# Gated FFN after a long convolution: gate activations written over the product's buffer, front loads on other queues, a row add on GpSimd

## The chip, the cores and the metric

One Trainium2 chip, one of its cores. The time is the device time of one execution in microseconds, as the median of several runs. The engines are PE (matrix products), ACT (activations, and reads of PSUM), DVE (elementwise work), POOL (GpSimd: here small elementwise work and DMA issues) and SP (DMA issues alone). Every engine works through its own list of instructions in order and waits for the others on semaphores.

## The reference

```python
def _A_ref(q, k, v, shift_k, ssm_k, ssm_D):          # B, S, D = 1, 2048, 640
    k_shift = sum over t < 4 of k shifted by t, times shift_k[:, t]
    kv = k_shift * v
    y = causal long convolution of kv with ssm_k, along S, by FFT of length 2 S
    y = y + kv * ssm_D
    return q * y

def _B_ref(x, w_gate, w_up, w_down):                 # F = 1728
    return (silu(x @ w_gate) * (x @ w_up)) @ w_down

h = A_q + _A_ref(layernorm(A_q), A_k, A_v, A_shift_k, A_ssm_k, A_ssm_D)
out = h + _B_ref(layernorm(h), B_w_gate, B_w_up, B_w_down)
```

## The kernel before

The sequence is cut into four blocks j = 0 to 3 of 512 rows, held as four rows b per partition, and the channels into two halves c of 320. Each block goes through the convolution half by half, then a layer norm, then the FFN. `block_j` (L1151) says the work of one block.

**Convolution.** `kv_block` (L926) makes kv on DVE: eight instructions of 128x1280 per half, on loads kin (of A_k) and vin (of A_v). `k_natural` (L621) transposes the filter: twelve PE transposes at L633 (called ktr below) of the load kraw (of A_ssm_k), one evacuation of 1280 columns, and for block 0 one add of a 320-element row, ssm_D, into the filter's first row (L640, called dadd): that is the skip term. Block 0 uses dense tables (`dense_c`, L690, tables den loaded in pieces by SP). Its forward products on PE are df (with an evacuation each), its inverse products di. Blocks 1 to 3 use a two-stage transform: s1 and s2 on PE (`fwd`, with a shuffle by DMA in between), products of spectra on DVE (`products`), an inverse i2 on PE (`inv2`), again a shuffle by DMA, and the last inverse i1 in `conv_bp` (L1009), which also multiplies by q, adds x and takes the statistics of the layer norm. Block j multiplies spectra of all blocks up to j, so the DVE work grows with j.

**Layer norm of h.** `ln_dve` aggregates the statistics on DVE, `ln_rstd` (L859) finds the inverse root; for j > 0 by fourteen Newton instructions of 128x4 and a last product at L887, all on POOL. `norm` (L890) writes the normalised rows, and `ln_bp` (L1056) transposes them with twenty PE instructions at L1068 (called tr).

**FFN.** `ffn_pair` (L1093) works on two of the 14 feature blocks of F: ten matmuls of 512 columns for the gate (tile pg) and ten for the up projection (tile pu). ACT applies SiLU to pg into the SBUF tile sg (L1107), and DVE multiplies pu by sg into GUT. In the last pair gate and up of the half-filled feature block share one group, so that it has ten matmuls and five. pg and pu come out of one PSUM pool, pF, of two slots; sg has one slot. `ffn_b` (L1130) does the down projection of a row group b, as three pieces of matmuls of 320 columns into PSUM of the same pool (called dn), evacuates and stores it.

**What sets the order.** Nothing is issued in the order of the code. `Prog.schedule` (L104) simulates the five engines with a cost for each operation, takes on each engine the ready operation of lowest priority number, and hands out pool slots as they come free. The lists it makes are the program. Every DMA is put on the list of a named engine, and its landing is set by `dma_model` (L1188), which keeps a clock for the transfers of SP and ACT and another, `bulk`, for those of POOL. An operation may reserve a tile that it doesn't write: it is then scheduled only once that tile has a slot, but its engine doesn't wait for it. The gate groups reserve sg in this way, and the up groups reserve the cells of GUT.

**Names of a step.** A number after a name is block, half, and piece: ktr01 is block 0, half 1; dn125 is block 1, row group 2, feature blocks from 5; i221h2 is the inverse of block 2, half 1, piece 2.

## Time and profile before

| | |
|---|---|
| median of 3 runs | 372.04 us (370.67 to 372.58) |
| the profiled execution's own time | 370.17 us |
| its span, first to last instruction | 368.4 us |
| PE busy | 314.0 us, 85% |
| DVE busy | 223.6 us, 61% |
| ACT busy | 205.8 us, 56% |
| POOL busy | 65.6 us, 18% |
| granted TensorE clock, mean | 0.943 |

All times below are from the start of the span. A timeline row gives start, duration, engine, line, operation, output and input with their shapes, and how many instructions it merges; the bracket at its end is the idle time of the engine before it, and what ended it. q after an engine's name means that its sequencer issued a DMA.

### The profile page before, as it was taken

To read this page: it belongs to the slowest core of one execution; us is meant where nothing else is said; L and a number is where in the kernel's file an instruction comes from. 1 tells how busy PE (TensorE), PEld (TensorE's weight loads), DVE (VectorE), ACT (ScalarE), POOL (GpSimd) and SP (SyncE) were. 2 spreads that over 40 slices of the span, in tenths; PEclk is the share of its full clock that TensorE was granted. 3 is DMA by queue.
4 is the path that set the end of the run, shared out by engine and by line. 5 is a ranking of instruction groups with operands and counts; after the bars stand their busy time and mean duration, and the time that the engine had idled before them with its cause. 6 is when DMAs were issued, how large, how long until landed. Compare 5 with 4: busy or idle time off the path is not lost.

```text
span 368.4 us, 5392 instructions
## 1 busy us (share of the span) xinstructions
PE 314.0 (85%) x2005; PEld 168.1 (46%) x2024; DVE 223.6 (61%) x365; ACT 205.8 (56%) x322; POOL 65.6 (18%) x145
## 2 busy tenths in 40 slices
PE   2599786699999999599888998669998999877993
PEld 0267452345445566244333664244453565333561
DVE  1388787867777785768989968741873701221200
ACT  4278989966676652877763555488763233122111
POOL 3222244361111007000510000600410020000000
PEclk9999998689999999789999999559999999999997
DMA  8997558605414213421200323402001011000011
GB/s 236 359 366 233 157 192 238 224 36 183 130 51 156 97 66 106 155 78 42 96 0 2 117 63 125 162 36 107 2 36 37 0 37 36 2 0 0 0 37 36
DMA packets 22013, 37.16 MB, mean 101 GB/s; under 512 B 2616, under 2 KB 17363, under 8 KB 21988
## 3 DMA queue, kind: packets, MB, share of 16 engines
q1 hardware_dynamic: 16116, 19.51, 14.9%
q0 software_dynamic: 3968, 15.98, 13.8%
q10 hardware_dynamic: 1904, 1.34, 1.3%
q8 instruction: 16, 0.26, 0.3%
q14 instruction: 9, 0.07, 0.1%
HBM read 22.40 MB, written 2.62 MB: 68 GB/s over the span
## 4 chain that ended last, share of the span: by engine, by line
PE 71%; ACT 12%; DMA 4%; POOL 3%; issue 3%; DVE 3%; ACTq 1%; DVEq 0%; POOLq 0%
PE ps L549 68%; ACT sb L534 4%; ACT sb L1107 4%; PE ps L633 3%; DMA sb<-in_A_ssm_k_dram 3%; ACT sb L895 3%; DVE sb L754 2%; DMA sb<-sb 1%; ACTq L542 1%; PE ps L1068 1%; POOL stt L880 1%; POOL stt L879 1%; ACT sb L914 1%; POOL sb L542 1%; POOL stt L881 1%
## 5 line engine op out<-in xcount | busy, mean ns | idle before, releaser
L549 PE MATMUL ps<-sb 128*128 128x320 bf16 (+3 forms) x1207 | 229.4, 338 | 18.8 <-ACT sb L1107 11.2
L754 DVE TENSOR_TENSOR sb<-sb 128x1280 bf16<-128x1280 bf16 (+2 forms) x250 | 161.2, 686 | 35.1 <-ACT sb L534 11.6
L549 PEld LDWEIGHTS ps<-sb 128*128 128x128 bf16 (+2 forms) x1226 | 113.8, 98 | 116.8 <-issue 17.4
L534 ACT ACTIVATE sb<-ps 128x640 bf16<-128x640 f32 (+2 forms) x155 | 109.3, 740 | 86.5 <-PE ps L549 67.3
L549 PE MATMUL ps<-sb,tab 128*64 128x320 bf16 (+2 forms) x622 | 79.8, 330 | 14.6 <-ACT sb L534 9.1
L754 DVE TENSOR_TENSOR sb<-ps,sb 128x1024 bf16<-128x1024 f32 (+3 forms) x44 | 44.4, 1016 | 56.1 <-ACT sb L1107 28.3
L549 PEld LDWEIGHTS ps<-sb,tab 128*64 128x64 f16 (+2 forms) x622 | 39.4, 106 | 54.0 <-issue 21.7
L1107 ACT ACTIVATE sb<-ps 128x1024 bf16<-128x1024 f32 (+2 forms) x32 | 29.3, 917 | 50.7 <-PE ps L549 50.1
L895 ACT ACTIVATE sb<-sb,stt 128x320 bf16<-128x320 bf16 (+1 forms) x42 | 27.8, 710 | 4.4 <-POOL stt L887 3.5
L537 ACT ACTIVATE sb<-ps 128x640 bf16<-128x640 f32 x24 | 16.1, 699 | 10.1 <-PE ps L549 9.8
L633 PE MATMUL ps<-sb 128*128 128x128 bf16 (+1 forms) x96 | 13.7, 240 | 8.3 <-DMA sb<-in_A_ssm_k_dram 8.3
L874 POOL TENSOR_SCALAR stt<-stt 128x4 f32<-128x4 f32 x6 | 2.6, 428 | 84.3 <-DVE stt L856 42.4
L633 PEld LDWEIGHTS ps<-sb 128*128 128x128 bf16 (+1 forms) x96 | 8.6, 117 | 14.8 <-DMA sb<-in_A_ssm_k_dram 9.0
L542 POOL DMA_DIRECT2D sb<-in_A_v_dram x6 | 4.7, 780 | 54.4 <-PE ps L549 53.2
L852 DVE BATCH_NORM_STATS2 stt<-sb 128x6 f32<-128x320 bf16 x32 | 14.0, 480 | 0.0
L542 POOL DMA_DIRECT2D sb<-in_A_ssm_k_dram x12 | 7.7, 647 | 31.3 <-PE ps L633 31.3
L914 ACT ACTIVATE sb<-sb,stt 128x640 bf16<-128x640 bf16 x16 | 13.2, 824 | 0.0
L1068 PE MATMUL ps<-sb 128*128 128x128 bf16 x80 | 7.4, 269 | 6.4 <-ACT sb L537 5.0
L907 ACT ACTIVATE sb<-sb 128x640 bf16<-128x640 bf16 x16 | 11.8, 736 | 0.0
L1068 PEld LDWEIGHTS ps<-sb 128*128 128x128 bf16 x80 | 6.5, 123 | 8.0 <-ACT sb L537 5.9
L542 POOL DMA_DIRECT2D sb<-in_A_k_dram x6 | 5.8, 975 | 19.0 <-DVE sb L754 17.4
L894 DVE TENSOR_SCALAR sb<-sb,stt 128x640 bf16<-128x640 bf16 x6 | 2.5, 443 | 10.3 <-POOL stt L887 10.3
(30 smaller groups left out, 64.5 us busy)
## 6 DMA issues: line engine op xcount, KB each, us to landing
sb<-sb SPq DMA_DIRECT2D x72, 160.0 KB, 2.2
sb<-in_A_k_dram POOLq DMA_DIRECT2D x6, 560.0 KB, 4.9
out_dram<-sb SPq DMA_DIRECT2D x16, 160.0 KB, 1.8
sb<-cst_den SPq DMA_DIRECT2D x9, 256.0 KB, 8.7
sb<-in_B_w_gate_dram POOLq DMA_DIRECT2D x5, 416.0 KB, 4.2
sb<-in_B_w_up_dram POOLq DMA_DIRECT2D x5, 416.0 KB, 4.3
sb<-in_A_q_dram POOLq DMA_DIRECT2D x3, 640.0 KB, 4.8
sb<-in_A_v_dram POOLq DMA_DIRECT2D x6, 320.0 KB, 3.5
```

The lines of the kernel that those rows point to most:

```text
L534: fns = {"act": lambda a: a.activation(out=dst(), in_=src(), func=ACTF.Copy), "dve": lambda v: v.tensor_copy(out=dst(), in_=src())}
L537: fns = {"act": lambda a: a.activation(out=dst(), in_=src(), func=ACTF.Copy, scale=scale), "dve": lambda v: v.tensor_scalar(out=dst(), in0 ...
L542: fns = [(lambda g, d=d, s=s: g.dma_start(d(), s())) for d, s in subs]
L549: return lambda t: t.matmul(o(), l(), r(), start=st, stop=sp)
L633: return t.transpose(B16(pt, b // 2, (b % 2) * CW + d * 128, pr), src, V(IDN, 0, pr, 0, pr))
L754: return lambda v: v.tensor_tensor(out=o(), in0=a(), in1=b_(), op=op)
L852: vec(dve1(CW, False), lambda v: v.bn_stats(st6(l, j, b, c), V(xt, b * D + c * CW, CW)), [(xt, (b, c))], [(ST, ("s", l, j, b, c))], prio, ...
L895: "act": lambda a: a.activation(out=dst(), in_=src(), func=ACTF.Identity, scale=rs(l, j, b), bias=tmv(l, j, 3)[:, b:b + 1])},
L907: P.op({"act": act_c(D) + 0.22}, lambda a, b=b, jt=jt: a.activation(out=V(jt, 0, D), in_=V(xt, b * D, D), func=ACTF.Copy, accum_out=tmv(l, ...
L914: P.op({"act": act_c(D) + 0.3}, lambda a, b=b, jt=jt: a.activation(out=V(jt, 0, D), in_=V(xt, b * D, D), func=ACTF.Square, bias=tmv(l, j, ...
L1068: fns.append(lambda t, k=k, d=d: t.transpose(B16(pt, k, d * 128, 128), V(hn[k], d * 128, 128), V(IDN, 0, 128)))
L1107: P.op({"act": act_c(n)}, lambda a: a.activation(out=dst(), in_=src(), func=ACTF.Silu), rd, wr, -1000, name=f"si{j}{i}")
```

## The change

**The buffer.** The pool of sg is gone. SiLU writes its result straight into the cells of GUT that the product will fill, and the product is formed in place. The gate groups reserve those cells, the up groups nothing.

**The loads.** vin of both halves of block 0 moves from ACT's list to SP's, and kraw of the second half too. The load of x for block 1 (640 KB, on POOL) now comes after the last DVE instruction of the first `kv_block`.

**The row add.** dadd moves from DVE to POOL.

**The model.** `dma_model` has one clock for all large transfers, at 370 KB per us, and a fixed cost for the shuffles. It moves no instruction by itself, but it gives other landing times, so the lists of all engines come out otherwise.

```diff
...
@@ -507,7 +507,6 @@
         P.pool("P0", [HNT.base + i * 2 * CW for i in range(4)], True)
         P.pool("EP", slots(4, 2 * CW), True)
         P.pool("JK", slots(1, 2 * CW), True)
-        P.pool("SG", slots(1, 1024), True)
         P.pool("pF", [0, 1024])
         P.pool("pC", [2048, 3072])
 
@@ -599,7 +598,7 @@
                 subs = [rows(0, 128)]
             dma(subs, 573, [], [(kt, 0)], prio, name=f"kin{j}{c}", eng="pool" if j else "sp")
             dma([(lambda: V2(vt, 0, CW, 4, CW), lambda: dram(V2d, B * j * D + c * CW, [[R * D, 128], [D, 4], [1, CW]]))],
-                328, [], [(vt, 0)], prio + 1, name=f"vin{j}{c}", eng="pool" if j else "act")
+                328, [], [(vt, 0)], prio + 1, name=f"vin{j}{c}", eng="pool" if j else "sp")
 
         def load_kraw(j, c, prio):
             if (j, c) == (0, 1):
@@ -609,12 +608,12 @@
             base = c * CW * S + B * j
             dma([(lambda: V2(t, 0, B, 2, B), lambda: dram(A_ssm_k, base, [[S, 128], [128 * S, 2], [1, B]])),
                  (lambda: V(t, 2 * B, B, 0, 64), lambda: dram(A_ssm_k, base + 256 * S, [[S, 64], [1, B]]))],
-                328, [], [(t, 0)], prio, name=f"kraw{j}{c}", eng="pool" if j else "act")
+                328, [], [(t, 0)], prio, name=f"kraw{j}{c}", eng="pool" if j else ("sp" if c else "act"))
 
         def load_x(j, prio):
             t = xts[j] = P.tile(f"x{j}", "XH")
             dma([(lambda: V(t, 0, 4 * D), lambda: dram(X2, B * j * D, [[R * D, 128], [1, R * D]]))], 655, [],
-                [(t, (b, c)) for b in range(4) for c in range(2)], prio, name=f"x{j}", eng="pool" if j else "sp")
+                [(t, (b, c)) for b in range(4) for c in range(2)], prio, name=f"x{j}", eng="pool" if j else "sp", after=[kv_last[0, 0]] if j == 1 else ())
 
         kts = {}
 
@@ -637,9 +636,9 @@
             evac(lambda: V2(kt, 0, 2 * CW, 2, 2 * CW), lambda: B16x2(pt, 2 * CW), 4 * CW, [(pt, 0)], [(kt, 0)], prio, fast=True,
                  name=f"kte{j}{c}")
             if j == 0:
-                vec(0.25, lambda v: v.tensor_tensor(out=V(kt, 0, CW, 0, 1), in0=V(kt, 0, CW, 0, 1),
-                                                    in1=V(DROW, c * CW, CW, 0, 1), op=ALU.add),
-                    [(DROW, 0), (kt, 0)], [(kt, 0)], prio, name="dadd")
+                P.op({"pool": 1.0}, lambda g: g.tensor_tensor(out=V(kt, 0, CW, 0, 1), in0=V(kt, 0, CW, 0, 1),
+                                                              in1=V(DROW, c * CW, CW, 0, 1), op=ALU.add),
+                     [(DROW, 0), (kt, 0)], [(kt, 0)], prio, name="dadd")
 
         def fwd(nm, srcs, pool, prio):
 
@@ -1094,7 +1093,6 @@
             fbs = (2 * i, 2 * i + 1)
             last = fbs[1] == 13
             g, u = P.tile("pg", "pF"), P.tile("pu", "pF")
-            sg = P.tile("sg", "SG")
             hr = [(HNT, (d, bp)) for d in range(5) for bp in range(2)]
 
             def group(t, bank, w, st, col, cell, prio, reserve):
@@ -1110,22 +1108,22 @@
                 vec(dve1(n), tt(dst, src, sgv, ALU.mult), rd, wr, -1000, name=f"gm{j}{i}")
 
             f0, f1 = fbs
-            group(g, 0, WG, FM, f0 * 128, 0, pf + 4 * i, [(sg, 0)])
+            group(g, 0, WG, FM, f0 * 128, 0, pf + 4 * i, [(GUT, f0)])
             if not last:
-                group(g, 1, WG, FM, f1 * 128, 1, pf + 4 * i + 1, [(sg, 1)])
-                group(u, 0, WU, FM, f0 * 128, 0, pf + 4 * i + 2, [(GUT, f0)])
-                group(u, 1, WU, FM, f1 * 128, 1, pf + 4 * i + 3, [(GUT, f1)])
-                silu(lambda: V2(sg, 0, 512, 2, 512), lambda: B32x2(g, 512), 1024, [(g, 0), (g, 1)], [(sg, 0), (sg, 1)])
-                mul(lambda: V2(GUT, f0 * 512, 512, 2, 512), lambda: B32x2(u, 512), lambda: V2(sg, 0, 512, 2, 512), 1024,
-                    [(u, 0), (u, 1), (sg, 0), (sg, 1)], [(GUT, f0), (GUT, f1)])
+                group(g, 1, WG, FM, f1 * 128, 1, pf + 4 * i + 1, [(GUT, f1)])
+                group(u, 0, WU, FM, f0 * 128, 0, pf + 4 * i + 2, [])
+                group(u, 1, WU, FM, f1 * 128, 1, pf + 4 * i + 3, [])
+                silu(lambda: V(GUT, f0 * 512, 1024), lambda: B32x2(g, 512), 1024, [(g, 0), (g, 1)], [(GUT, f0), (GUT, f1)])
+                mul(lambda: V2(GUT, f0 * 512, 512, 2, 512), lambda: B32x2(u, 512), lambda: V2(GUT, f0 * 512, 512, 2, 512), 1024,
+                    [(u, 0), (u, 1), (GUT, f0), (GUT, f1)], [(GUT, f0), (GUT, f1)])
             else:
-                group(g, 1, GUL, 128, 0, 1, pf + 4 * i + 1, [(sg, 1), (GUT, f1)])
-                group(u, 0, WU, FM, f0 * 128, 0, pf + 4 * i + 2, [(GUT, f0)])
-                silu(lambda: V(sg, 0, 512), lambda: B32(g, 0, 512), 512, [(g, 0)], [(sg, 0)])
-                silu(lambda: V(sg, 512, 512, 0, 64), lambda: B32(g, 1, 512, 64, 128), 512, [(g, 1)], [(sg, 1)])
-                mul(lambda: V(GUT, f1 * 512, 512, 0, 64), lambda: B32(g, 1, 512, 0, 64), lambda: V(sg, 512, 512, 0, 64), 512,
-                    [(g, 1), (sg, 1)], [(GUT, f1)])
-                mul(lambda: V(GUT, f0 * 512, 512), lambda: B32(u, 0, 512), lambda: V(sg, 0, 512), 512, [(u, 0), (sg, 0)], [(GUT, f0)])
+                group(g, 1, GUL, 128, 0, 1, pf + 4 * i + 1, [(GUT, f1)])
+                group(u, 0, WU, FM, f0 * 128, 0, pf + 4 * i + 2, [])
+                silu(lambda: V(GUT, f0 * 512, 512), lambda: B32(g, 0, 512), 512, [(g, 0)], [(GUT, f0)])
+                silu(lambda: V(GUT, f1 * 512, 512, 0, 64), lambda: B32(g, 1, 512, 64, 128), 512, [(g, 1)], [(GUT, f1)])
+                mul(lambda: V(GUT, f1 * 512, 512, 0, 64), lambda: B32(g, 1, 512, 0, 64), lambda: V(GUT, f1 * 512, 512, 0, 64), 512,
+                    [(g, 1), (GUT, f1)], [(GUT, f1)])
+                mul(lambda: V(GUT, f0 * 512, 512), lambda: B32(u, 0, 512), lambda: V(GUT, f0 * 512, 512), 512, [(u, 0), (GUT, f0)], [(GUT, f0)])
 
         def ffn_b(j, b, pf):
             xt = xts[j]
@@ -1185,17 +1183,17 @@
             block_j(j)
 
 
+        link = [1.4]
+
         def dma_model(o, issued, dmafree):
             kb, shuffle = o.dma
-            if o.eng == "pool":
-                s = max(issued + 1.2, bulk[0])
-                bulk[0] = s + kb / 200.0
-                return bulk[0] + 1.1
-            s = max(issued + 0.9, dmafree[0])
-            dmafree[0] = s + kb / (150.0 if shuffle else 330.0)
-            return dmafree[0] + 1.1
-
-        bulk = [0.0]
+            if shuffle:
+                s = max(issued + 0.4, dmafree[0])
+                dmafree[0] = s + 0.55
+                return s + 2.2
+            s = max(issued + (1.2 if o.eng == "pool" else 0.8), link[0])
+            link[0] = s + kb / 370.0
+            return link[0] + 1.0
 
         P.schedule(0.12, dma_model, 1.0)
         if _INFO is not None:
```

The lists stand here at three places, before and after. Lines of the changed kernel are lower by one or two. First POOL at the front, before: the load of x for block 1, then kraw of block 1 (two transfers), kin of block 1, the first weights, vin.

```order
L595 MEMSET sb 1x960 x2
L542 DMA sb<-in_A_q_dram 128x2560
L542 DMA sb<-in_A_ssm_k_dram 128x2x512
L542 DMA sb<-in_A_ssm_k_dram 64x512
L542 DMA sb<-in_A_k_dram 128x7x320
L542 DMA sb<-in_B_w_gate_dram 128x1664
L542 DMA sb<-in_B_w_up_dram 128x1664
L542 DMA sb<-in_A_v_dram 128x4x320
```

The first thing that POOL does after the memsets is the load of x for block 1. The changed list, from the same memset:

```order
L594 MEMSET sb 1x960 x2
L541 DMA sb<-in_A_ssm_k_dram 128x2x512
L541 DMA sb<-in_A_ssm_k_dram 64x512
L639 ISA
L639 TENSOR_TENSOR sb<-sb 1x320
L541 DMA sb<-in_A_k_dram 128x7x320
L541 DMA sb<-in_B_w_gate_dram 128x1664
L541 DMA sb<-in_B_w_up_dram 128x1664
L541 DMA sb<-in_A_q_dram 128x2560
L541 DMA sb<-in_A_v_dram 128x4x320
```

The load of x has moved behind the first weights; ISA (a change of POOL's library) and the first dadd stand behind kraw of block 1.

The second place is PE in the FFN of block 3, its last two pairs; s_act is ACT's semaphore and s_dve that of DVE. Before:

```order
L549 MATMUL ps<-sb 128x512 [waits s_act]
L549 MATMUL ps<-sb 128x512 x9
L549 MATMUL ps<-sb 128x512 [waits s_dve]
L549 MATMUL ps<-sb 128x512 x9
L549 MATMUL ps<-sb 128x512 [waits s_act]
L549 MATMUL ps<-sb 128x512 x4
L549 MATMUL ps<-sb 128x512 [waits s_dve]
L549 MATMUL ps<-sb 128x512 x9
L549 MATMUL ps<-sb 128x320 [waits s_dve]
```

The group of five is the last up group, so up stands ahead of gate in each pair from the second on: the up group waits for the SiLU of the pair before, the gate group for its product. The changed list at the same place:

```order
L548 MATMUL ps<-sb 128x512 [waits s_act]
L548 MATMUL ps<-sb 128x512 x9
L548 MATMUL ps<-sb 128x512 [waits s_dve]
L548 MATMUL ps<-sb 128x512 x9
L548 MATMUL ps<-sb 128x512 [waits s_act]
L548 MATMUL ps<-sb 128x512 x9
L548 MATMUL ps<-sb 128x512 [waits s_dve]
L548 MATMUL ps<-sb 128x512 x4
L548 MATMUL ps<-sb 128x320 [waits s_act,s_dve]
```

Gate now stands ahead of up, the group of five is the last, and each gate group waits for the SiLU of the pair before, each up group for its product.

The third place is PE at the end of the convolution of block 2. Rows of 128x320 out of sb alone are down projections of block 1; of 128x320 with tab, inverses; of 64x320, spectra of block 3. From i221h2 to the transposes at L1068, before:

```order
L549 MATMUL ps<-sb,tab 128x320 x16
L549 MATMUL ps<-sb 128x320 x12
L549 MATMUL ps<-sb,tab 64x320 x6
L549 MATMUL ps<-sb 128x320 x10
L549 MATMUL ps<-sb,tab 64x320 x4
L549 MATMUL ps<-sb 128x320 x8
L549 MATMUL ps<-sb,tab 128x320 x8
L549 MATMUL ps<-sb,tab 64x320 x24
L549 MATMUL ps<-sb,tab 128x320 x24
L1068 MATMUL ps<-sb 128x128 x20
```

Between i221h2 and i1210 (the row of eight with tab) stand thirty down projection matmuls. The changed list, from the last down projection:

```order
L548 MATMUL ps<-sb 128x320 x8
L548 MATMUL ps<-sb,tab 128x320 x34
L548 MATMUL ps<-sb,tab 64x320 x10
L548 MATMUL ps<-sb,tab 128x320 x8
L548 MATMUL ps<-sb,tab 64x320 x24
L548 MATMUL ps<-sb,tab 128x320 x12
L1067 MATMUL ps<-sb 128x128 x20
```

All down projections now stand ahead; the row of 34 ends with the sixteen matmuls of i221h2 and i221h3, and only ten matmuls follow before i1210. Twelve of the 24 matmuls of i230 have gone behind the transposes.

## Rows read from the trace of the kernel before

**Rows 1.** The page: span, PE's busy time, and its granted clock in 40 slices

```profile
span 368.4 us, 5392 instructions
...
PE 314.0 (85%) x2005; PEld 168.1 (46%) x2024; DVE 223.6 (61%) x365; ACT 205.8 (56%) x322; POOL 65.6 (18%) x145
...
PEclk9999998689999999789999999559999999999997
```

**Rows 2.** PE's waits, by releaser: us in total, times, longest

```profile
PE ps L549 <- ACT sb L1107: 11.2, 11, 1.1
```

**Rows 3.** Busy time by stretch: length, then busy PE PEld DVE ACT POOL, clock, DMA

```profile
155.64:201.19 45.55, 41.20 (x216) 18.41 (x220) 37.48 (x54) 28.55 (x49) 6.60 (x16) 0.96 0.13 47
...
226.69:248.58 21.89, 13.79 (x102) 7.83 (x102) 14.64 (x30) 14.59 (x24) 6.47 (x16) 0.61 0.31 106
```

**Rows 4.** Timeline of the front: PE, ACT and DVE around the first transposes

```profile
10.08 2.09 PE L633 MATMUL ps<-sb 128*128 128x128 bf16 x12 [5.25 <-DMA sb<-in_A_ssm_k_dram]
...
12.21 1.24 ACT L534 ACTIVATE sb<-ps 128x1280 bf16<-128x1280 bf16 x1 [3.17 <-PE ps L633]
...
13.55 0.31 DVE L640 TENSOR_TENSOR sb<-sb 1x320 bf16<-1x320 bf16 x1 [2.61 <-ACT sb L534]
...
15.21 2.09 PE L633 MATMUL ps<-sb 128*128 128x128 bf16 x12 [3.04 <-DMA sb<-in_A_ssm_k_dram]
...
17.24 2.74 PE L549 MATMUL ps<-sb 128*128 128x320 bf16 x12
...
20.32 18.20 PE L549 MATMUL ps<-sb 128*128 128x320 bf16 x132 [0.34 <-ACT sb L534]
```

**Rows 5.** DMA issues: engine, count, KB each, median us from issue to landing

```profile
sb<-sb SPq DMA_DIRECT2D x72, 160.0 KB, 2.2
...
sb<-in_A_v_dram ACTq DMA_DIRECT2D x1, 320.0 KB, 5.8
...
sb<-in_A_ssm_k_dram ACTq DMA_DIRECT2D x1, 64.0 KB, 7.4
```

**Rows 6.** Timeline of ACT's queue at the start

```profile
1.17 0.75 ACTq L542 DMA_DIRECT2D sb<-in_A_v_dram  x1
1.96 1.16 ACTq L542 DMA_DIRECT2D sb<-in_A_ssm_k_dram  x2
```

**Rows 7.** POOL's library change, by line: duration min/median/max in ns, first and last start

```profile
L887 POOLq MODIFY_POOL_CONFIG  x2: 37/37/37, 35.4 to 35.4; - x2
```

**Rows 8.** Timeline of POOL: first arithmetic, then the layer norm of block 1

```profile
39.00 0.68 POOL L887 TENSOR_TENSOR stt<-stt 128x4 f32<-128x4 f32 x1 [3.58 <-DVE stt L869]
...
139.04 1.31 POOL L542 DMA_DIRECT2D sb<-in_A_ssm_k_dram  x2 [2.64 <-PE ps L633]
...
142.31 0.76 POOL L881 TENSOR_SCALAR stt<-stt 128x4 f32<-128x4 f32 x1
```

**Rows 9.** Timeline of PE, block 1: transposes after the layer norm

```profile
151.29 1.48 PE L1068 MATMUL ps<-sb 128*128 128x128 bf16 x20 [3.16 <-ACT sb L537]
```

**Rows 10.** Timeline of PE, end of block 2's convolution: i221, i121, i230, transposes

```profile
219.82 1.37 PE L549 MATMUL ps<-sb,tab 64*128 64x320 bf16 x15
...
226.54 1.26 PE L549 MATMUL ps<-sb,tab 128*128 128x320 bf16 x8
...
236.39 3.38 PE L549 MATMUL ps<-sb,tab 64*128 64x320 bf16 x24 [1.19 <-DVE sb L754]
241.64 2.31 PE L1068 MATMUL ps<-sb 128*128 128x128 bf16 x20 [1.87 <-ACT sb L537]
```

**Rows 11.** Timeline of ACT there: evacuations of i221h2 and i221h3

```profile
220.74 1.29 ACT L537 ACTIVATE sb<-ps 128x640 bf16<-128x640 f32 x2
```

**Rows 12.** Timeline of the FFN of block 3: SiLU on ACT, PE, product on DVE

```profile
322.88 1.02 ACT L1107 ACTIVATE sb<-ps 128x1024 bf16<-128x1024 f32 x1 [4.58 <-PE ps L549]
323.96 4.49 PE L549 MATMUL ps<-sb 128*128 128x512 bf16 x20 [1.12 <-ACT sb L1107]
324.00 1.23 DVE L754 TENSOR_TENSOR sb<-ps,sb 128x1024 bf16<-128x1024 f32 x1 [4.38 <-ACT sb L1107]
```

## What is forecast, before the changed kernel ran

> **What bounds the kernel now.** I read the page first [rows 1]: PE is busy 314.0 of 368.4 us, and the change adds and takes no matmul. So the time can only come from PE's 54 idle us and from the stretches in which its clock is granted at less than full. The list of PE's idle times, in order of time, shows them in five places. The reader should look in each for what ended the wait, since that is what the change must touch.
>
> First the front. PE transposes the filter of block 0 at 10.08 after 5.25 us idle, then stands 3.04 us more for the second half's filter (ktr01 at 15.21), and its long run of dense products begins at 17.24 [rows 4]. Second, the SiLU waits: 11.2 us in 11 times, longest 1.1 [rows 2]. Third, the transposes behind the layer norm of block 1, 3.16 us [rows 9]. Fourth, the end of block 2's convolution, where PE is busy 13.79 of 21.89 us at a mean granted clock of 0.61 [rows 3]; two levels, 1.2 and 2.4 GHz, stand behind that mean. Fifth, many short waits between 39 and 74 us for evacuations by ACT, which the change does not aim at.
>
> **SiLU waits.** The timeline of the last FFN shows how one arises [rows 12]: ACT starts a SiLU at 322.88, PE starts its twenty matmuls at 323.96 after 1.12 us idle, and only then DVE's product runs. Twenty matmuls take 4.49 us, so a pair takes 5.61. The order says why. sg had one slot, so the scheduler could not place the next gate group before the product had freed it; it placed the next up group, which needs the PSUM slot that the SiLU has yet to read. Without sg, gate comes first in every pair. A gate group waits for the SiLU of the pair before, which now has the up group beside it: ten matmuls, half of 4.49, 2.25 us against 1.02 of SiLU [rows 12]. An up group waits for the product, 1.23 us, which has the gate group beside it. Both waits are hidden. The tail of block 3 has five waits of 1.12: **-5.6**. Its last wait, for the product ahead of the first down projection, is not among them and stays. The other six of the eleven sum to 11.2 - 5.6 = 5.6. Four of them lie in 155.64:201.19, where PE is idle 4.35 us in all [rows 3]; I take **-3.8** there and **-1.8** for the two after 248. Bounds for the tail: -5.6, if nothing else is late, and -4.5, if one of the five is replaced by a late product.
>
> In place, SiLU and product write the same number of elements as before, at the same cost. SiLU now also waits for the down projections of the block before, which read those cells; but they stand ahead of the gate group on PE's in-order list, so that wait is over when the gate group's own is. Nothing is queued behind it.
>
> **Front.** kraw of the first half goes out at 1.96 behind vin on ACT's queue [rows 6], and its second transfer, issued at 2.61, lands 7.4 us later [rows 5]: that is PE's start at 10.08. In the change kraw is where vin was. The 320 KB of vin, issued at 1.17, landed after 5.8 us, at 7.0 [rows 5, 6]; kraw has the same 320 KB, and 640 KB of x for block 1 no longer run beside it. So 6.9, with bounds 5.5 and 8.1. From there: transposes 2.09, evacuation 1.24 [rows 4], and dadd. On DVE dadd took 0.31; on POOL a 128x4 instruction took up to 0.76 beside a busy DVE [rows 8]. I take 0.6, and the first dense product at 6.9 + 2.1 + 1.3 + 0.6 = 10.9, against 17.24. What hid there: in the old order ktr01 stood ahead of all dense products and held them until its own load had landed; now it stands behind 76 of them.
>
> Not all of 6.3 us stays. Up to the first inverse product, di0h0, the new list has 36 filter products and 32 of kv: twelve of the first kind until 20.32 - 17.24 = 3.08 us on, the other 56 at 18.20/132 = 0.138 each, 7.7; so 10.9 + 10.8 = 21.7. The old one had twelve and 48: 17.24 + 3.08 + 6.62 = 26.94. The gain is 5.2 there; the new list has then done eight filter products more (1.1) but still owes the twelve of ktr01 (1.4), so 4.9. DVE is ahead too: it was blocked 2.61 us by dadd [rows 4], and no longer is. Against it: the second dadd stands on POOL behind kraw of block 1, which cannot be issued before ktr10 has read its buffer. Issue 1.31 [rows 8] and dadd 0.6 come to 1.9 us, under which PE has one group of eight matmuls, 1.1: 0.8 lost, as PE's next filter products wait for it. Left over, 4.1. From 20 to 74 us ACT and DVE carry the pace, and both shift with their inputs. I take **-4.1**, bounds -7 (DVE's lead counts as well) and +0.6 (kraw at 8.1, and the 3.5 us of the next lines).
>
> POOL's first arithmetic came at 39.00, 3.5 us behind the library change at 35.4, and it had waited for DVE all that time [rows 7, 8]; so the trace bounds the cost of the first use between nothing and 3.5 us. I take nothing: the row starts as its wait ends. The Trainium skill ("GPSIMD Engine Reference", 2.1 Instruction dispatch) says that the first call of a freshly loaded library pays some 6 us that no row shows. No row here reaches that; by it the sum would be 6 us higher.
>
> **Block 1's layer norm.** POOL's Newton chain stood 2.64 us behind the issue of kraw, which waits for ktr30 on PE [rows 8]. The new list has nine Newton instructions ahead of that issue, so the wait is filled, though the issue still waits. PE's 3.16 us [rows 9] shrink by between 0 and 2.64: **-1.3**.
>
> **Block 2's end gives back.** The third place in the order matters here. PE reaches i221h2 earlier by 4.1 + 1.3 + 3.8, but with thirty more down projections ahead, 30 x 0.138 = 4.1: 5.1 earlier, so i221h3 ends at 221.19 - 5.1 = 216.1 [rows 10]. What used to hide the next step is gone. The evacuations end 0.84 us behind i221h3 [rows 11], the shuffle takes 2.2 [rows 5], with issue 3.3 in all; ten matmuls cover 1.4 of it. So i1210 comes at 219.4, not 226.54, and its pair ends at 220.7, not 227.8. From there to the transposes it took 13.84 us [rows 10] for statistics, Newton chain and norm. In the new list i230h0 stands ahead of the transposes, and two evacuations of 0.65 [rows 11] must free its slot first: 15.1. Transposes at 235.8, 5.8 earlier than 241.64, with twelve matmuls of i230 still to do (half of 3.38 at that clock, 0.85 at the full one; I take 0.9). So 4.9 is left of 9.2: **+4.3**. Bounds: 0, if the clock is granted in full there, and +8, if DVE's products for i221h2 are late as well and the low clock lasts longer.
>
> **Sum.** -4.1 - 1.3 - 3.8 + 4.3 - 1.8 - 5.6 = -12.3. The profiled execution took 370.17 (its span is 368.4), so 357.9; it lay 1.9 below the median of 372.04. Against the median: 359.7, say **360**.
>
> **Rivals.**
> 1. *The library change is paid on the path.* It stands just ahead of the first dadd, for which PE waits. At the trace's bound of 3.5 us the first dense product comes at 14.4, the front brings 0.6 instead of 4.1, and the time is 363.5. For it: between 35.4 and 39.00 POOL did no other arithmetic, so a load could have lain there unseen. Against it: the row at 39.00 starts as its input comes [rows 7, 8]. The page named above ("GPSIMD Engine Reference", the Trainium skill) would make it 366.
> 2. *Block 2 gives nothing back.* PE works on other stages while the chain runs, or the chain was bound by PE's lower clock: 360 - 4.3 = 355, with DVE's lead at the front 352. For it: the wait at 0.61 of the clock [rows 3] may go altogether. Against it: the order leaves ten matmuls there.
> 3. *The front is hidden anyway.* ACT and DVE bind until 74 us on work that hangs on later loads (x, the den tables), now behind more bytes of SP's queue. Then the front brings nothing, and block 2 takes the FFN gain: -1.8 - 5.6 + about 1, so 366. If the tail's waits also return as late products, it ends within 0.5% of 372.
> 4. *Slower: the chains at the ends of blocks 1 to 3 stand bare.* All three have fewer down projections behind the last inverse. The place is i221h3 to the transposes: the 20.5 us of before (221.19 to 241.64) with the ten, eight, sixteen, and twelve matmuls left there, at half clock. If i221h2 waits for DVE too, +8 there, +2 each at blocks 1 and 3, and 5 more as matmuls run at the lower level: +17. With the front at +0.6 and -12.5 of the other gains that is 377. It decides once it outruns all gains, 16.6: PE would stand some 25 us in that stretch instead of 8.1 [rows 3].
>
> **How the numbers follow.** Forecast 0.5 (356 to 364); rival 1 0.12; rival 2 0.13 (351 to 356); rival 3 0.18, of which 0.08 within 0.5% of the median; rival 4 0.07. The range 352 to 369 leaves out rival 4, the same-as-before part of rival 3 and the end of rival 2, some 0.18. Half a per cent, 1.9 us, is about what a measurement of this kernel tells from no change. So faster 0.85, same 0.08, slower 0.07.
>
> **What would show it.** In the profile after, PE's waits for L1107 must all but vanish (11.2 us now), and the last FFN's pairs must take 4.5 us. The first dense product must stand near 11 us, directly behind dadd on POOL; a gap of several us between POOL's library change and dadd is rival 1. The stretch from the last down projection of block 1 to block 2's transposes must show more idle PE than 8.1 us. If it doesn't, the +4.3 was wrong; if the tail keeps its 1.12 us waits, the reading of the order was.

## The result, and the profile after

The changed kernel takes **360.32 us** (358.12 to 363.30) against 372.31 for the kernel before beside it: a ratio of 0.969, 95% interval 0.961 to 0.978. That is 12.0 us, faster by far more than the half per cent that a measurement tells apart. The profiled execution is the longest of its four: 363.3 us, span 361.3. Lines of the changed kernel are lower by one or two, so L1107 (SiLU) is now L1105, and L887 is L886. In the medians and ratios of this document an execution more than 1.5% above the fastest of its kernel is left out: one of e6_combo, and one of the kernel before, beside e1_buffer to e4_dadd.

The page of the changed kernel, in the lines that answer to [rows 1]:

```profile
span 361.3 us, 5379 instructions
...
PE 314.9 (87%) x2005; PEld 168.1 (47%) x2024; DVE 225.4 (62%) x366; ACT 203.0 (56%) x319; POOL 68.5 (19%) x147
...
PEclk9998997559999999999999999558999999999997
```

PE is as busy as before: what went is idle time. PE's waits after, by releaser (us in total, times, longest):

```profile
PE ps L548 <- ACT sb L533: 14.8, 19, 2.3
PE ps L548 <- POOL sb L639: 5.1, 2, 3.0
PE ps L1067 <- ACT sb L536: 3.5, 2, 2.8
PE ps L548 <- DVE sb L753: 3.2, 6, 1.0
PE ps L1067 <- ACT sb L533: 3.2, 1, 3.2
PE ps L548 <- DMA sb<-sb: 2.6, 1, 2.6
```

No row names L1105: the 11.2 us of [rows 2] are gone. At the front one row is new, POOL's additions (L639), and one has grown: PE waited 1.4 us for the transposes of block 0's layer norm before, and waits 3.2 now. To see where the time went, the span is cut at five places: first FFN product of block 0, of block 1, i221h2, the transposes of block 2, first FFN product of block 3. Each row gives the stretch, its length, then busy time (and instructions) of PE, PEld (PE's weight loads), DVE, ACT, POOL, the granted clock as a share of the full one, and of the DMA engines the busy share and the GB/s. The kernel before:

```profile
0.00:74.16 74.16, 51.94 (x342) 31.34 (x344) 51.69 (x103) 54.03 (x94) 23.59 (x41) 0.93 0.77 249
74.16:155.64 81.48, 76.46 (x517) 40.85 (x523) 61.47 (x95) 51.81 (x74) 19.96 (x42) 0.96 0.33 109
155.64:219.67 64.03, 59.68 (x361) 30.23 (x364) 52.95 (x76) 39.35 (x65) 7.40 (x17) 0.97 0.17 60
219.67:241.64 21.97, 14.79 (x115) 7.72 (x115) 18.07 (x36) 12.55 (x22) 6.47 (x16) 0.75 0.34 120
241.64:307.36 65.72, 62.57 (x413) 33.76 (x420) 30.75 (x50) 37.16 (x58) 8.23 (x30) 0.95 0.10 36
307.36:368.40 61.04, 48.52 (x260) 24.23 (x261) 8.72 (x8) 10.86 (x13) 0.00 (x0) 0.96 0.05 17
```

The changed kernel, cut at the same operations:

```profile
0.00:75.69 75.69, 53.49 (x339) 31.55 (x341) 50.25 (x97) 51.13 (x87) 25.08 (x42) 0.87 0.74 244
75.69:157.07 81.38, 78.27 (x521) 41.09 (x527) 63.18 (x101) 54.00 (x80) 21.62 (x42) 0.97 0.30 103
157.07:220.62 63.55, 62.27 (x392) 33.02 (x396) 53.28 (x77) 39.00 (x65) 8.20 (x18) 1.00 0.21 72
220.62:242.87 22.25, 10.54 (x71) 3.97 (x71) 16.95 (x34) 15.18 (x29) 6.46 (x16) 0.64 0.31 108
242.87:308.33 65.46, 64.15 (x433) 34.44 (x440) 33.11 (x52) 33.22 (x49) 7.14 (x30) 0.97 0.11 38
308.33:361.30 52.97, 46.17 (x252) 24.06 (x253) 8.63 (x8) 10.44 (x13) 0.00 (x0) 0.96 0.05 16
```

Length less busy PE is PE's idle time. It is the measure to compare, since matmuls have also moved between stretches:

| stretch | idle before | idle after | change | predicted |
|---|---|---|---|---|
| up to the first FFN product | 22.2 | 22.2 | 0.0 | -4.1 |
| FFN of block 0, layer norm of block 1 | 5.0 | 3.1 | -1.9 | -1.3 |
| FFN of block 1 | 4.4 | 1.3 | -3.1 | -3.8 |
| end of block 2's convolution | 7.2 | 11.7 | +4.5 | +4.3 |
| FFN of block 2 | 3.2 | 1.3 | -1.8 | -1.8 |
| FFN of block 3 | 12.5 | 6.8 | -5.7 | -5.6 |

Five of the six terms came out within 0.8 us. The front did not: in this execution it brought nothing.

Idle time tells the tail too small. These are two SiLUs of the changed kernel's last FFN:

```profile
323.42 1.02 ACT L1105 ACTIVATE sb<-ps 128x1024 bf16<-128x1024 f32 x1 [3.29 <-PE ps L548]
...
327.73 1.02 ACT L1105 ACTIVATE sb<-ps 128x1024 bf16<-128x1024 f32 x1 [3.29 <-PE ps L548]
```

A pair now takes 4.31 us; before, with 1.12 idle and 4.49 busy, it took 5.61 [rows 12]. So each wait cost 1.30 us and not 1.12: in the trace a matmul of 512 columns lasts 0.38 us and the next one starts 0.22 us behind it, so in the 4.49 the end of the last one, which no other overlaps, counts as busy. Over five waits that is 6.5 us for a forecast of 5.6.

The experiments ask two things: is the gain of the FFNs really the order of the groups, and what became of the front.

### The profile page after: what moved, and what is told of

Same layout as the page of the kernel before. It is cut to its first block, busy times and chain, and to the rows that moved or that the text cites. A ratio compares the mean times of both kernels' runs of the same rounds, so it can differ in the third digit from the quotient of the medians.

```text
span 361.3 us, 5379 instructions
## 1 busy us (share of the span) xinstructions
PE 314.9 (87%) x2005; PEld 168.1 (47%) x2024; DVE 225.4 (62%) x366; ACT 203.0 (56%) x319; POOL 68.5 (19%) x147
## 4 chain that ended last, share of the span: by engine, by line
PE 69%; DMA 9%; ACT 6%; DVE 5%; POOL 5%; issue 4%; ACTq 0%; POOLq 0%; DVEq 0%
PE ps L548 65%; DVE sb L753 4%; PE ps L632 3%; ACT sb L533 3%; DMA sb<-in_B_w_down_dram 2%; PE ps L1067 2%; DMA sb<-in_A_k_dram 2%; DMA sb<-in_A_ssm_k_dram 2%; DMA sb<-in_B_w_gate_dram 2%; ACT sb L894 1%; POOL sb L541 1%; DMA sb<-in_A_v_dram 1%; DMA sb<-in_B_w_up_dram 1%; POOL stt L880 1%; POOL stt L879 1%
## 5 line engine op out<-in xcount | busy, mean ns | idle before, releaser
L548 PEld LDWEIGHTS ps<-sb 128*128 128x128 bf16 (+2 forms) x1226 | 115.2, 99 | 110.7 <-issue 17.1
L533 ACT ACTIVATE sb<-ps 128x640 bf16<-128x640 f32 (+2 forms) x152 | 106.2, 730 | 91.9 <-PE ps L548 74.0
L548 PE MATMUL ps<-sb,tab 128*64 128x320 bf16 (+2 forms) x622 | 81.2, 326 | 17.4 <-ACT sb L533 11.7
L548 PEld LDWEIGHTS ps<-sb,tab 128*64 128x64 f16 (+2 forms) x622 | 38.2, 105 | 58.9 <-issue 28.0
L1105 ACT ACTIVATE sb<-ps 128x1024 bf16<-128x1024 f32 (+2 forms) x32 | 29.3, 915 | 37.2 <-PE ps L548 37.0
L1067 PE MATMUL ps<-sb 128*128 128x128 bf16 x80 | 7.5, 266 | 6.7 <-ACT sb L536 3.5
L534 DVE COPY sb<-ps 128x1280 bf16<-128x1280 bf16 x4 | 3.3, 824 | 12.1 <-PE ps L1067 12.1
L1067 PEld LDWEIGHTS ps<-sb 128*128 128x128 bf16 x80 | 6.4, 122 | 8.6 <-ACT sb L536 4.5
```

What stands on the lines that cost most here:

```text
L533: fns = {"act": lambda a: a.activation(out=dst(), in_=src(), func=ACTF.Copy), "dve": lambda v: v.tensor_copy(out=dst(), in_=src())}
L548: return lambda t: t.matmul(o(), l(), r(), start=st, stop=sp)
L1067: fns.append(lambda t, k=k, d=d: t.transpose(B16(pt, k, d * 128, 128), V(hn[k], d * 128, 128), V(IDN, 0, 128)))
L1105: P.op({"act": act_c(n)}, lambda a: a.activation(out=dst(), in_=src(), func=ACTF.Silu), rd, wr, -1000, name=f"si{j}{i}")
```

## Experiments

The kernels and their medians; each ratio is against runs of the kernel before on the same chip.

| kernel | median, us | ratio (95%) |
|---|---|---|
| e1_buffer: before, buffer part alone | 364.62 | 0.980 (0.975 to 0.984) |
| e2_front: all but the buffer part | 368.40 | 0.989 (0.984 to 0.994) |
| e12_reserve: before, only sg's reservation dropped | 365.24 | 0.981 (0.976 to 0.986) |
| e9_wait: after, the old wait put back | 359.09 | 0.968 (0.963 to 0.972) |
| e5_again: after, unaltered | 360.36 | 0.969 (0.965 to 0.973) |
| e7_kraw31: before, one load moved | 369.77 | 0.994 (0.991 to 0.997) |
| e3_nm: after, one step ahead of a load | 358.56 | 0.964 (0.960 to 0.968) |
| e4_dadd: after, additions ahead of loads | 358.28 | 0.963 (0.959 to 0.968) |
| e6_combo: both | 356.38 | 0.957 (0.953 to 0.962) |
| e10_vec: after, additions back to DVE, new order | 359.34 | 0.967 (0.963 to 0.972) |
| e8_dve: e3_nm, additions on DVE, order kept | 355.31 | 0.955 (0.950 to 0.959) |
| e11_wd: e8_dve, weights held back | 358.32 | 0.963 (0.959 to 0.967) |

Where one instruction moves, the list of an engine is altered after `P.schedule`, so that everything else stays in its place:

```diff
+def place(e, name, n, ahead, m):      # n-th of `name` goes ahead of m-th of `ahead`
+    L = P.order[e]
+    o = [x for x in L if x.name == name][n]
+    L.remove(o)
+    L.insert(L.index([x for x in L if x.name == ahead][m]), o)
     ...
```

### The two halves of the change

e1_buffer has the diff's part in `ffn_pair` and the pool SG alone; e2_front has everything else.

> The kernel before with the gate buffer alone changed; loads, skip term and DMA model stay as before. Theory A (what the trace of after shows): the front of the change brings nothing by 75 us, and the whole gain comes from the buffer. Then this kernel is as fast as the changed one, 358 to 363 us, its first FFN1 product starts at 74.2 us as before, and no product waits for a SiLU (11.2 us before). Theory B (the prediction's sum): 4.1 us of the gain are the front's and 0.7 us more come with it, so this kernel stands about 4 to 5 us above the changed one, 364 to 366 us.

> The changed kernel with the separate gate buffer put back; loads, skip term on GpSimd and DMA model as in the changed one. Theory A: the first dense product comes about 4.7 us earlier than before (12.5 against 17.24), but the first FFN1 product is not earlier than before (75.7 against 74.16), so the time is 371 to 374 us. Theory B: the front's gain reaches the end, 366 to 368 us.

By time the parts add: 372.50 - 364.62 = 7.9 us for the buffer, 372.50 - 368.40 = 4.1 (2.3 to 5.8 by its interval) for the rest, 12.0 together, as much as both. Theory A, formed on the one trace, fell: the front part does gain. But in e2_front's trace little of it at the front: its first FFN product stands at 73.27, 0.9 us ahead of before, and the next stretch, which ends with block 1's layer norm, is 78.37 us instead of 81.48. Of these 3.1 us 1.6 are idle PE (3.4 instead of 5.0), and 1.5 are busy PE, at a granted clock of 1.00 instead of 0.96.

### Wait or order?

The prediction said that sg made the SiLU waits through the order of the groups. Two kernels split the two. e9_wait keeps the changed kernel's lists and gives each SiLU its old wait for the product of the pair before:

```diff
+for j in range(4):
+    for i in range(1, 7):
+        for s in byname[f"si{j}{i}"]:
+            for g in byname[f"gm{j}{i - 1}"]:
+                s.deps[g] = max(s.deps.get(g, 0), 1)
```

e12_reserve keeps sg in the kernel before, and drops the reservation, in the same way in the last pair:

```diff
-group(g, 0, WG, FM, f0 * 128, 0, pf + 4 * i, [(sg, 0)])
+group(g, 0, WG, FM, f0 * 128, 0, pf + 4 * i, [])
 ...
-group(g, 1, WG, FM, f1 * 128, 1, pf + 4 * i + 1, [(sg, 1)])
+group(g, 1, WG, FM, f1 * 128, 1, pf + 4 * i + 1, [])
```

> The changed kernel, every instruction in its place, with the old wait put back alone: each SiLU waits for the products of the pair before it, as it did when all pairs shared one gate buffer. If the removed wait is worth what the row of the kernel before says (11.2 us in front of FFN products, 5.6 of them in the last block): 368 to 371 us, with the five waits of 1.12 us in the last block back. If outside the last block the waits fall beside other work: 5.6 us alone, 366 us. If the order of instructions and not the wait makes the gain: 360 to 361 us.

> The kernel before with the separate gate buffer kept and only its reservation taken away: the gate groups no longer reserve sg, so they may be scheduled before it is free; loads, skip term and model stay as before. If the gain of the buffer part is the order of the groups (gate ahead of up in each pair, so that a SiLU runs beside its up group): the five waits of 1.12 us in the last block go and the time is that of the kernel with the buffer alone changed, 363 to 366 us. If the shared buffer itself made the waits: 371 to 373 us.

The wait costs nothing (359.09 against 360.3), and dropping the reservation, with the buffer still separate and still one slot, gives the whole gain of the buffer part (365.24 against 364.62). The last FFN of e12_reserve, in rows like [rows 12]:

```profile
321.78 9.44 PE L549 MATMUL ps<-sb 128*128 128x512 bf16 x43
...
322.62 1.02 ACT L1107 ACTIVATE sb<-ps 128x1024 bf16<-128x1024 f32 x1 [3.29 <-PE ps L549]
324.78 1.23 DVE L754 TENSOR_TENSOR sb<-ps,sb 128x1024 bf16<-128x1024 f32 x1 [3.09 <-PE ps L549]
```

PE runs through; SiLU is followed by its product 2.16 us later, when the up group has come, and not at once as in [rows 12]. Gate first is what gains here. Writing over GUT saves a buffer, and no time that these runs could tell.

### Is the front's gain there at all?

> The changed kernel once more, unaltered. Its first profiled execution was the longest of its four (363.3 us) and reached the first FFN1 product at 75.69 us, 1.5 us behind the kernel before; the same front in the kernel with the separate gate buffer reached it at 73.27. Theory C: the stretch up to FFN1 differs by 2 to 4 us between executions of one order, everything behind it hardly; then this execution spends 285 to 286 us from the first FFN1 product to the end, as the first one did (285.6), wherever that product starts, and it starts at 71 to 74 us. Theory A (the front gains nothing): it starts at 75 to 76 us again. Time by both 358 to 363 us.

e5_again starts its first FFN product at 74.63 and takes 285.8 us from there to the end; the first execution took 285.6, e9_wait 283.8. Up to that product e2_front, e5_again and e9_wait have the changed kernel's lists, and e1_buffer, e7_kraw31 and e12_reserve those of before. So there are four executions of each front: before 74.16, 74.76, 77.69 and 78.06, mean 76.2; after 75.69, 74.63, 73.27 and 72.75, mean 74.1. **The means differ by 2.1 us, half of the 4.1, but one execution of a front differs from the next by 3 to 4 us, and the two ranges overlap.** Counted as idle PE they hardly do: 22.2 to 23.5 us before, 20.5 to 22.2 after, and the means differ by 1.4. A third estimate comes from e2_front: it is 4.1 us faster by time, and from its first FFN product to its end takes 291.9 us against 294.2 of before, so 1.8 are left for the front. The three agree on a gain of about 2 us; none is clear of the spread by itself. The two traces that I compared first were a short one of before and the longest of after. Part of the spread shows in the clock. e9_wait's front, in a row as above:

```profile
0.00:72.75 72.75, 52.25 (x339) 31.21 (x339) 49.43 (x95) 50.76 (x86) 25.09 (x42) 0.91 0.76 253
```

The same lists in the first execution took 75.69 us, at a mean clock of 0.87 and with 53.49 us of busy PE. The two long fronts of before, e1_buffer and e12_reserve, have 54.6 us of busy PE for the work that takes 51.9 and 52.2 in the short ones. Idle time differs as well (20.5 in e9_wait's front, 22.2 in the first execution's), so the clock isn't all; what else it is stays open.

### Where the other half of the front went

Block 0's second layer norm in the changed kernel, from the reciprocal (L868) to the transposes (L1067):

```profile
62.21 0.30 DVE L868 RECIPROCAL stt<-stt 128x4 f32<-128x4 f32 x1
...
65.84 0.72 POOL L541 DMA_DIRECT2D sb<-in_B_w_down_dram  x1 [3.30 <-DMA sb<-in_B_w_down_dram]
...
66.57 0.21 POOL L886 TENSOR_TENSOR stt<-stt 128x4 f32<-128x4 f32 x1
...
66.88 3.35 ACT L894 ACTIVATE sb<-sb,stt 128x640 bf16<-128x640 bf16 x4 [2.71 <-POOL stt L886]
...
70.88 1.36 PE L1067 MATMUL ps<-sb 128*128 128x128 bf16 x11 [3.22 <-ACT sb L533]
```

The last step of the norm (L886, called nm10: the second norm, block 0) had its input at 62.5 and ran at 66.57. Ahead of it on POOL's list stands the issue of a down-weight load, which waited 3.30 us for the landing of an earlier one. And at the front:

```profile
7.37 2.09 PE L632 MATMUL ps<-sb 128*128 128x128 bf16 x12 [2.45 <-DMA sb<-in_A_ssm_k_dram]
...
9.49 1.24 ACT L533 ACTIVATE sb<-ps 128x1280 bf16<-128x1280 bf16 x1 [3.43 <-PE ps L632]
10.12 1.46 POOL L541 DMA_DIRECT2D sb<-in_A_ssm_k_dram  x2 [7.47 <-PE ps L632]
...
11.67 0.78 POOL L639 TENSOR_TENSOR sb<-sb 1x320 bf16<-1x320 bf16 x1
...
12.51 1.78 PE L548 MATMUL ps<-sb 128*128 128x320 bf16 x6 [3.05 <-POOL sb L639]
...
29.16 1.27 POOL L541 DMA_DIRECT2D sb<-in_A_ssm_k_dram  x2 [4.33 <-PE ps L632]
...
30.45 1.30 POOL L639 TENSOR_TENSOR sb<-sb 1x320 bf16<-1x320 bf16 x1
...
31.81 1.61 PE L548 MATMUL ps<-sb 128*128 128x320 bf16 x7 [2.03 <-POOL sb L639]
```

The evacuation ends at 10.73, but POOL issues kraw of block 1 until 11.6, and only then adds. So e3_nm, e4_dadd and both:

```diff
+place("pool", "nm10", 0, "wd", 3)         # e3_nm, e6_combo
+place("pool", "dadd", 0, "kraw10", 0)     # e4_dadd, e6_combo
+place("pool", "dadd", 1, "kraw11", 0)     # e4_dadd, e6_combo
```

> The changed kernel with one instruction moved one place: on GpSimd the last step of block 0's second layer norm (nm10) stands ahead of the fourth down-weight load instead of behind it. Theory A: the step ran at 66.57 us because the load ahead of it waited until 65.84 for another load's landing, while its own input was there at 62.5. Moved, it runs by 62.7, the transposes behind it start at 67.5 instead of 70.88, the first FFN1 product at 72.3 instead of 75.69, and the time falls by 2 to 3.5 us. Rival: the shuffles of the same stretch (landing at 66.0 to 68.9) set the pace, and the time stays within 0.5 us.

> The changed kernel with the two skip-term additions on GpSimd moved ahead of the filter loads (kraw10 and kraw11) that stand before them. The first dense product then starts at 11.6 us instead of 12.51, and the 2.03 us wait before the dense product at 31.81 goes. Theory A: this gain is lost again at the layer norm at 66.6 us that waits for a weight load, so the time moves by 0 to -0.5 us. Rival: the earlier start is kept through block 0, and the time falls by 2 to 3 us.

> The changed kernel with both edits of the runs before: the layer norm's last step ahead of the fourth down-weight load, and the two skip-term additions ahead of the filter loads. If the two waits lie in series on the path, the gains add: 1.8 from the one and 2.0 from the other against 360.3 us, so 356.0 to 357.0 us, with the wait of about 3.2 us ahead of the first transposes of block 0's second layer norm down to 1.5. If the second wait only takes over what the first gives back, 358 us as with either alone.

Alone each gives about 2 us with an interval that overlaps the changed kernel's, so neither is settled alone; together they give 4.0, and 0.957 (0.953 to 0.962) stands apart from 0.969 (0.965 to 0.973). That is what two waits in series would give. My own expectation for e4_dadd, that its gain would be lost again at nm10, is not what the median says. e3_nm's trace has the step at 61.54, 5 us earlier than in the changed kernel's, and the wait at the transposes at 1.49:

```profile
61.54 0.35 POOL L886 TENSOR_TENSOR stt<-stt 128x4 f32<-128x4 f32 x1 [0.34 <-DVE stt L868]
...
67.13 2.10 PE L1067 MATMUL ps<-sb 128*128 128x128 bf16 x18 [1.49 <-ACT sb L533]
```

### Which engine adds the skip term?

e10_vec undoes the dadd hunk of the diff and lets the scheduler place the additions on DVE; e8_dve keeps the lists, has nm10 as in e3_nm, and puts the additions on DVE where their input has just come:

```diff
+place("pool", "nm10", 0, "wd", 3)
+to_dve(0, "kva00", 1)        # first dadd: off POOL's list, on DVE ahead of the second kva00
+to_dve(1, "m2003", 0)        # second dadd
```

> The changed kernel with one part undone: the skip-term additions go to VectorE again and the order is worked out anew with them there (VectorE takes the first one third in its row, ahead of its input, and waits). If the addition on GpSimd is what the new front needs: VectorE waits some 2 us early, as it did before (2.61 us), and the time is 362 to 365 us. If the earlier filter load makes the gain by itself: the first dense product at 10.9 us, and 358 to 360 us.

> The changed kernel with the layer norm's last step ahead of the fourth down-weight load, and both skip-term additions on VectorE, at places where their input has just come (behind the fourth product of the first value group, and between the complex products of block 0), instead of GpSimd. If GpSimd is worth its price: 0.3 us more on VectorE twice delays its chain, so 357 to 358 us. If its slower addition (0.78 and 1.08 us against 0.31) and the slowdown of VectorE beside it (1.41 against 0.83 us for one product) cost more: the first dense product at 10.9 us instead of 11.4, and 355.5 to 356.5 us.

e10_vec: 359.34, no slower than the changed kernel, though DVE waits 2.03 us ahead of its addition. So the earlier filter load and the new order carry the front, not GpSimd. e8_dve is the fastest of all, 355.31; against e6_combo that is 1.1 us, with intervals that overlap, so which engine adds is not settled by time. Its addition takes 0.31 us and the first dense product comes at 10.85:

```profile
10.48 0.31 DVE L639 TENSOR_TENSOR sb<-sb 1x320 bf16<-1x320 bf16 x1
...
10.85 3.38 PE L548 MATMUL ps<-sb 128*128 128x320 bf16 x12 [1.75 <-DVE sb L639]
```

### Block 1's layer norm, and a failed try

e7_kraw31 is the kernel before with the load that [rows 8] show inside the Newton chain moved behind it.

```diff
+place("pool", "kraw31", 0, "x2", 0)
```

> The kernel before with one load moved: the last filter load (kraw31) stands behind block 1's layer norm on GpSimd instead of inside it (GpSimd waited 2.64 us for it at 139.04 and spent 1.30 us issuing it). The prediction's step: the wait of 3.16 us ahead of block 1's transposes shrinks and gives 1.3 us, 371 us. Rival: the whole wait and the stretch at the low clock behind it go, 4 to 4.5 us, 368 us, as the stage from FFN1's end to the next block's first FFN1 product went from 31.9 to 27.3 us in the kernel with the new front and the old buffer. Third: nothing, since the load was waited for in the shadow of other work, 372.5 us.

It gives 2.1 us (1.0 to 3.3 by the interval), between the two readings. PE's wait of 3.16 us [rows 9] shrinks to 2.02, and the stretch has 3.2 us of idle PE, close to the 3.1 of the changed kernel:

```profile
150.74 1.33 PE L1068 MATMUL ps<-sb 128*128 128x128 bf16 x20 [2.02 <-ACT sb L537]
```

This prices the load in the old list. It does not show that the load alone made the gain of the changed kernel, whose PE list differs there too: its twenty transposes stand in two runs of ten with other products around them, the longest wait is 0.70, and e1_buffer, which has the old loads and such runs of ten, also has only 2.4 us of idle PE in this stretch.

e11_wd is e8_dve with nm10 moved further forward, past two more weight loads, and the load vin11 past one, to free the DMA engines for the shuffles of block 0:

```diff
-place("pool", "nm10", 0, "wd", 3)
+place("pool", "vin11", 0, "wd", 1)
+place("pool", "nm10", 0, "wd", 1)
```

> The changed kernel with the additions on VectorE as in the fastest version so far (355.3 us), and the layer norm's last step now ahead of the second to fourth down-weight loads, so that these start after it and not beside the shuffles of block 0. Theory: the shuffles, which took 6.4 us from issue to landing there against 2.1 us where no load ran beside them, land by 57 us, the wait of 2.4 us ahead of the products behind them goes, and the time is 353 to 354 us. Rival: the value load of block 1 beside them (vin11) is what slows them, or VectorE and ScalarE are next, and the time stays at 355 us.

The shuffles did become faster. The rows give KB and median us from issue to landing, of e8_dve and then of e11_wd:

```profile
sb<-sb SPq DMA_DIRECT2D x4, 160.0 KB, 6.6
```

```profile
sb<-sb SPq DMA_DIRECT2D x4, 160.0 KB, 3.9
```

PE's wait there fell from 2.38 to 0.22 us, but the wait ahead of the transposes grew from 0.58 to 3.00. First e8_dve, then e11_wd:

```profile
60.40 0.74 PE L548 MATMUL ps<-sb,tab 128*64 128x320 bf16 x4 [2.38 <-ACT sb L894]
...
62.65 1.57 PE L1067 MATMUL ps<-sb 128*128 128x128 bf16 x13 [0.58 <-ACT sb L533]
```

```profile
59.80 1.40 PE L548 MATMUL ps<-sb,tab 128*64 128x320 bf16 x8 [0.22 <-DMA sb<-sb]
...
64.20 2.10 PE L1067 MATMUL ps<-sb 128*128 128x128 bf16 x18 [3.00 <-ACT sb L533]
```

The time rose to 358.32, with an interval apart from that of e8_dve. Up to the first FFN product PE was idle about as long (15.0 against 15.5 us) but busy longer, 53.65 against 51.25 us at a mean clock of 0.89 against 0.92. The theory that the shorter wait would be the gain fell. Why the median is 3 us higher stays open. The clock of these two executions does not explain it: over the six executions of each kernel the mean granted clock is 0.95 for both.

## Why the prediction was right, and where it was wrong

- **SiLU waits** (-5.6, -3.8, -1.8): right in cause, and near in size. Idle PE fell by 5.7, 3.1 and 1.8 in the three FFNs, and e9_wait and e12_reserve show the cause given, the order that the reservation forces. The price of a wait was taken too low, 1.12 us for 1.30: a pair was forecast at 4.5 us and takes 4.31.
- **Block 2 gives back** (+4.3): measured +4.5. The stretch behind i221h2 holds 10.54 instead of 14.79 us of PE work and is no shorter, 22.25 against 21.97. The trace carries it; no experiment put the down projections back, so the cause is argued and not shown. The transposes came at 242.87 and not at the forecast 235.8, but 5.6 of these 7.1 us were already missing at the first FFN product (75.69 for 74.16 - 4.1).
- **Block 1's layer norm** (-1.3): a little small, -1.9 in the trace, 2.1 by e7_kraw31 in the old list. The cause given, the load inside the chain, is one of two: the transposes in runs of ten were not foreseen.
- **Front** (-4.1): the direction was right as far as the spread lets one see, the size about twice too large. Its first step was near: kraw landed at 7.32 (6.9 forecast), the first dense product came at 12.51 (10.9). Of the 1.6 us between, 0.4 are the landing, 0.2 the addition (0.78 for 0.6), and 0.9 the issue of kraw10 ahead of it. I had counted that for the second addition and not for the first. At the second the wait was 2.03 for 0.8: 0.7 of the difference is the addition (1.30 for 0.6), the rest is about what the issue ahead of it lost, which starts at 29.16, 0.6 us behind the end of PE's transposes. The step that failed is "From 20 to 74 us ACT and DVE carry the pace": I did not look at POOL there. Its list held nm10 behind a load that waits, and with nm10 and the two additions moved e6_combo got 4.0 us back.
- **Rivals.** The library change cost nothing on the path: it stands at 11.6, and the addition starts at 11.67.

```profile
L639 POOLq MODIFY_POOL_CONFIG  x2: 37/37/37, 11.6 to 11.6; - x2
```

  The some 6 us that the Trainium skill ("GPSIMD Engine Reference", 2.1 Instruction dispatch) gives for the first call of freshly loaded code don't show here. Rival 2 fell with the +4.5. Rival 3 is near in size, as about half of the front is hidden, but not in cause: the waits that were found are POOL's, not those of ACT and DVE for later loads. Rival 4's +17 did not come: blocks 1 and 3 lost nothing.
- **The sum** of -12.3 met the -12.0 partly by luck: one term was 2 us too large, and the others together some 1 us too small. From the first FFN product to the end, before took 294.2 us in its one trace and three executions of the changed lists 285.6, 285.8 and 283.8, mean 285.0: 9.2 less, where I had forecast 8.2. With the 2.1 of the front that is 11.3 of the 12.0 measured; the last 0.7 is below what these executions agree to.

## What to carry to other kernels

A buffer that a list scheduler must reserve can cost time by the order that it forces, though no engine ever waits for it: drop the reservation first, then ask whether the buffer matters. A queue that both issues loads and does small arithmetic holds the arithmetic behind each load that waits; look for such a place, and put the arithmetic ahead: three small steps, each moved ahead of one load, gave 4.0 us here. And compare a stretch over several executions before building a theory on it: one trace of each kernel showed no gain at the front, where four of each point to about 2 us.

## What the hardware showed that was not expected

- **DVE slows beside POOL.** With POOL's addition (0.78 us) at 10.54 in e4_dadd, the slowest of six equal DVE products takes 1412 ns instead of 826 (duration min/median/max):

```profile
L753 DVE TENSOR_TENSOR sb<-sb x6: 824/826/1412, 8.8 to 13.8; 128x1280 bf16<-128x1280 bf16 x6
```

  The Trainium skill ("SBUF — State Buffer", SBUF: two separate sides) says that the two share a pair of ports, held by one for a whole instruction while the other waits. The 0.59 us agree in kind. In e8_dve, with the addition on DVE, the slowest of eleven such products at the front takes 826 ns.
- **Shuffles beside weight and value loads took three times as long**: 6.6 us for 160 KB in e8_dve against a median of 2.2 [rows 5] over the whole kernel before, and 3.9 in e11_wd, which has fewer weight loads beside them.
- **An order does not fix a time.** The same lists reached the same product at 72.75 and at 75.69 us, and at 74.16 and 78.06.
